# Moving the loads of batches 2 to 7 of a linear-attention + SiLU-MLP kernel from SyncE's queue to GpSimd's software queue

## The chip, the cores and the metric

One core of one Trainium2 chip. The metric is the device time of one launch in microseconds (us). Most executions of a kernel here agree within about 1%; every number compared below is from runs that were classed as fast, unless it says otherwise. A run of a version stands beside runs of the kernel before on the same chip.

A core has TensorE (PE in the profile; PEld is its weight load), VectorE (DVE), ScalarE (ACT), GpSimd (POOL) and SyncE (SP). A transfer is issued by one of these engines and is carried out by 16 DMA engines that all issuers share. Transfers issued by SyncE stand in one queue (q1 in the profile), those issued by GpSimd in another, the software queue (q0). A transfer lands when its completion is signalled; "issue to landing" runs from the start of its issue to that moment. A packet is one record of a DMA engine's work in the trace, with its queue, time and size.

## The reference

```
q, k, v: (8 batches, 8 heads, 576 rows, 64), float32
q_s = softmax of q over its last axis; k_s = softmax of k over the rows
kv  = einsum('bhsd,bhse->bhde', k_s, v)
x   = einsum('bhsd,bhde->bhse', q_s, kv)      # as 4608 rows of 512
h   = x @ w_in                                # 512 -> 2048
out = (h * sigmoid(h)) @ w_out                # 2048 -> 512, float32
```

## The kernel before

The tokens are worked in nine chunks of 512. `units` is a list of small pieces of matmul work (`mm1` for w_in, `mm2` for w_out); the attention work of batch `b` is placed into it at offsets from `begin[b]`. The order in which the code emits an engine's instructions is the order of that engine's program. The parts that matter:

```python
def load(b, name, src, ccs=None, eng=nc.sync):          # one of q, k, v: 1152 KB, rows of 2304 B
    if name not in st[b]:
        st[b][name] = ld.tile([128, NG, J * D], FP32, name=name)      # two buffers per name
    ...
    eng.dma_start(out=st[b][name][:, c, :], in_=x[:, c, :])

def tr_dma(b, eng):                                     # qT: the transposed exp(q), by DMA
    eng.dma_start_transpose(out=qt_tile(b)..., in_=st[b]["eq"]...)

# start: weights and batch 1 in GpSimd's queue (load_w1/load_w2: 1 MB float32 each, converted to bf16)
load_w1(0); load_w1(1); load_w2(0); load_w1(2)
load(1, "qt", q, eng=nc.gpsimd); load_w2(1); load_w1(3)
load(1, "kt", k, eng=nc.gpsimd); load_w2(2); load(1, "vt", v, eng=nc.gpsimd); load_w2(3)
...
def plan_attn(b, u, sm, vs, tp, ks, ox, eng=nc.gpsimd):
    # exp, sum and norm of q at u+sm[0:2] (norm on GpSimd), exp of k at u+sm[2:4], cast of v at u+vs
    ...
    plan(u + tp, lambda: tr_dma(b, nc.sync))
    if b == 1:
        plan(u + vs[0] + 1, lambda: load_behind(2))
    if b + 2 < B:
        at_ = u + max(tp, vs[1]) + 1
        plan(at_, lambda: [load(b + 2, *x) for x in (("qt", q), ("kt", k), ("vt", v))])
    # kv products at u+ks; xt(b, cc), the first users of qT(b), at u+ox
    ...
def load_behind(b):     # a one-element copy into the q tile: batch 2's loads must wait for the cast of v of batch 1
    st[b]["qt"] = ld.tile([128, NG, J * D], FP32, name="qt")
    nc.vector.tensor_copy(st[b]["qt"][0:1, 0, 0:1], vaug[(b - 1) % 2][0:1, J - 1, D:E1])
    for x in (("qt", q), ("kt", k), ("vt", v)):
        load(b, *x)
```

So SyncE's queue carries, in this order: batch 0's loads, the transpose of batch 1, the loads of batches 2 and 3, eight stores of chunk 0, the transpose of batch 2, the loads of batch 4, eight stores, and so on.

The softmax here doesn't subtract the row's maximum and nothing guards it: scores larger than these inputs give would overflow.

Of the kernel before, what the change touches and what calls it, by code (L numbers as in the profile page):

```python
# [8 lines left out]
FP32 = mybir.dt.float32  # L9
# [7 lines left out]
def kernel(  # L17
# [13 lines left out]
    nc = tc.nc  # L31
    B, H, S, D = q.shape
# [3 lines left out]
    J = S // P  # L36
    NG = H // 2
# [7 lines left out]
    E1 = D + 1  # L45
# [6 lines left out]
    vaug = [glob.tile([128, J, NG * E1], BF16, name=f"vaug{i}") for i in range(2)]  # L52
# [7 lines left out]
    ld = ctx.enter_context(tc.tile_pool(name="ld", bufs=2))  # L60
# [5 lines left out]

    st = [dict() for _ in range(B)]

    def load(b, name, src, ccs=None, eng=nc.sync):
        if name not in st[b]:  # L70
            st[b][name] = ld.tile([128, NG, J * D], FP32, name=name)
        x = src[b].rearrange("(g r) (p j) d -> g (r p) (j d)", r=2, j=J).rearrange("g x y -> x g y")
        c = slice(0, NG) if ccs is None else slice(2 * ccs, 2 * ccs + 2)
        eng.dma_start(out=st[b][name][:, c, :], in_=x[:, c, :])  # L74

    def jgd(t, cc):
        return t[:, 2 * cc:2 * cc + 2, :].rearrange("p g (j d) -> p j g d", d=D)
# [1 line left out]
    def exp(b, src, dst, cc):  # L79
        if dst not in st[b]:  # L80
            st[b][dst] = ap.tile([128, J, NG * D], BF16, name=dst)
        o = st[b][dst][:, :, cc * 128:(cc + 1) * 128].rearrange("p j (g d) -> p j g d", d=D)
        nc.scalar.activation(out=o, in_=jgd(st[b][src], cc), func=ACT.Exp)  # L83

    def vcast(b, cc, eng):
        o = vaug[b % 2].rearrange("p j (g e) -> p j g e", e=E1)[:, :, 2 * cc:2 * cc + 2, 0:D]
        if eng is nc.scalar:
            eng.copy(out=o, in_=jgd(st[b]["vt"], cc))  # L88
        else:
            eng.tensor_copy(o, jgd(st[b]["vt"], cc))  # L90

    def qsum(b, cc):
        if "zq" not in st[b]:
            st[b]["zq"] = ap.tile([128, 2, J, 2], FP32, name="zq")
            st[b]["rzq"] = ap.tile([128, 2, J, 2], FP32, name="rzq")
        e = st[b]["eq"][:, :, cc * 128:(cc + 1) * 128].rearrange("p j (g d) -> p j g d", d=D)
        nc.vector.reduce_sum(out=st[b]["zq"][:, cc], in_=e, axis=AX.X)  # L97
        nc.vector.reciprocal(out=st[b]["rzq"][:, cc], in_=st[b]["zq"][:, cc])

    def qnorm(b, cc, eng):  # L100
        e = st[b]["eq"][:, :, cc * 128:(cc + 1) * 128].rearrange("p j (g d) -> p j g d", d=D)
        r = st[b]["rzq"][:, cc]
        eng.tensor_tensor(  # L103
            out=e, in0=e, in1=r[:, :, :, None].to_broadcast([128, J, 2, D]), op=ALU.mult
        )
# [7 lines left out]
    def tr_dma(b, eng):  # L113
        eng.dma_start_transpose(
            out=qt_tile(b).rearrange("x j c y -> x (j c) y"),
            in_=st[b]["eq"].rearrange("x j y -> x (j y)"),
        )
# [20 lines left out]
    def kv(b, cc):  # L138
        t = [ps.tile([128, 512], FP32, name="kvps", tag="ring", bufs=PSB["ring"]) for _ in range(2)]
        st[b]["kvps", cc] = t  # L140
        for j in range(J):
            for r in range(2):
                nc.tensor.matmul(  # L143
                    out=t[r][:, 0:2 * E1],
                    lhsT=st[b]["ek"][r * P:(r + 1) * P, j, cc * 128:(cc + 1) * 128],
                    rhs=vaug[b % 2][r * P:(r + 1) * P, j, cc * 2 * E1:(cc + 1) * 2 * E1],
                    start=(j == 0),
                    stop=(j == J - 1),
                )

    def kvcopy(b, cc):
        for r in range(2):
            kp = st[b]["kvps", cc][r]
            rz = ap.tile([128, 2], FP32, name="rz", bufs=4)
            nc.vector.reciprocal(out=rz, in_=kp[:, D:2 * E1:E1])  # L155
            for g in range(2):
                h = slice(g * 64, (g + 1) * 64)
                nc.vector.tensor_scalar_mul(  # L158
                    out=kvn[b % 3][h, cc, r, :],
                    in0=kp[h, g * E1:g * E1 + D],  # L160
                    scalar1=rz[h, g:g + 1],
                )
# [3 lines left out]
    def xt(t, cc, tags=("ring", "ring"), dve=0):  # L166
        if t not in XT:
            XT[t] = mp.tile([128, NC, S], BF16, name="XT")
        for i, (off, size) in enumerate(part[t]):
            o1 = [  # L170
                ps.tile([128, TCH], FP32, name="o1", tag=tags[i], bufs=PSB[tags[i]])
                for _ in range(2)
            ]
            a = first = cut[t] + off
            while a < first + size:
                b, col = divmod(a, S)
                n = min(S - col, first + size - a)
                for g in range(2):
                    for r in range(2):
                        h = slice(g * 64, (g + 1) * 64)  # L180
                        nc.tensor.matmul(
                            out=o1[g][r * 64:(r + 1) * 64, a - first:a - first + n],
                            lhsT=kvn[b % 3][h, cc, r, :],
                            rhs=st[b]["qT"][h, col // P:(col + n) // P, cc, r * P:(r + 1) * P],
                        )
                a += n
            for g in range(2):
                x = XT[t][:, 2 * cc + g, off:off + size]
                if g < dve:
                    nc.vector.tensor_copy(x, o1[g][:, 0:size])  # L190
                else:
                    nc.scalar.copy(out=x, in_=o1[g][:, 0:size])  # L192
# [70 lines left out]
    for cc in range(2):  # L263
        load(0, "qt", q, cc)
    for cc in range(2):
        load(0, "kt", k, cc)
        load(0, "vt", v, cc)
# [7 lines left out]
    def load_w1(i):  # L275
        nc.gpsimd.dma_start(  # L276
            out=W1[:, :, i * FQ:(i + 1) * FQ],
            in_=w_in[:, i * FQ:(i + 1) * FQ].rearrange("(c p) f -> p c f", p=128),
        )

    def load_w2(i):
        nc.gpsimd.dma_start(  # L282
            out=W2[:, i * 4:(i + 1) * 4, :],
            in_=w_out[i * FQ:(i + 1) * FQ, :].rearrange("(fc p) o -> p fc o", p=128),
        )
# [3 lines left out]
    load_w1(1)  # L289
    load_w2(0)  # L290
    load_w1(2)
    load(1, "qt", q, eng=nc.gpsimd)
    load_w2(1)
    load_w1(3)
    load(1, "kt", k, eng=nc.gpsimd)
    load_w2(2)
    load(1, "vt", v, eng=nc.gpsimd)
    load_w2(3)

    wps = ps.tile([128, 512], FP32, name="wps", tag="ops", bufs=PSB["ops"])  # L300

# [43 lines left out]
    begin = {t: next(u for u, f in enumerate(units) if f[0] == ("mm1", t)) for t in range(NCH)}  # L345
    at = [[] for _ in units]

    def plan(u, f):
        at[u].append(f)

    def plan_attn(b, u, sm, vs, tp, ks, ox, eng=nc.gpsimd):



        for cc in range(2):
            plan(u + sm[cc], lambda cc=cc: exp(b, "qt", "eq", cc))
            plan(u + sm[cc] + 1, lambda cc=cc: (qsum(b, cc), qnorm(b, cc, nc.gpsimd)))
        for cc in range(2):
            plan(u + sm[2 + cc], lambda cc=cc: exp(b, "kt", "ek", cc))
            plan(u + vs[cc], lambda cc=cc: vcast(b, cc, eng))  # L360
        plan(u + tp, lambda: tr_dma(b, nc.sync))
        if b == 1:
            plan(u + vs[0] + 1, lambda: load_behind(2))
        if b + 2 < B:
            at_ = u + max(tp, vs[1]) + 1
            plan(at_, lambda: [load(b + 2, *x) for x in (("qt", q), ("kt", k), ("vt", v))])
        for cc in range(2):
            plan(u + ks[cc], lambda cc=cc: kv(b, cc))
            plan(u + ks[cc] + 1, lambda cc=cc: kvcopy(b, cc))
        for cc in range(2):  # L370
            plan(u + ox[cc], lambda cc=cc: xt(b, cc))

    def load_behind(b):

        st[b]["qt"] = ld.tile([128, NG, J * D], FP32, name="qt")
        nc.vector.tensor_copy(st[b]["qt"][0:1, 0, 0:1], vaug[(b - 1) % 2][0:1, J - 1, D:E1])
        for x in (("qt", q), ("kt", k), ("vt", v)):
            load(b, *x)

    V = nc.vector  # L380
    plan_attn(1, begin[1], (-20, -19, -11, -10), (-6, -5), -12, (-4, -3), (-2, 0), V)
    plan_attn(2, begin[2], (-23, -21, -18, -15), (-13, -12), -15, (-10, -7), (-5, -3))
    for b in range(3, B):
        plan_attn(b, begin[b], (-40, -36, -32, -28), (-34, -30), -20, (-15, -11), (-7, -4))
    for cc in range(2):
# [36 lines left out]
```

## Time and profile before

| | before |
|---|---|
| median of three runs | 296.51 us (296.35 to 297.26) |
| span of the profiled run | 294.7 us |
| TensorE busy | 281.8 us, 96% |
| GpSimd busy | 52.0 us, 18% |
| transpose of batch 1, issue to landing | 9.3 us |
| transposes of later batches | 4.7 to 4.9 us, that of batch 6 6.2 us |

The page of the kernel before. The strips cut the span into 40 slices of 7.4 us; a digit is the busy share in tenths, PEclk is the granted TensorE clock in tenths.

```profile
span 294.7 us, 4438 instructions
PE 281.8 (96%) x1682; PEld 132.6 (45%) x1682; DVE 164.1 (56%) x340; ACT 152.6 (52%) x250; POOL 52.0 (18%) x44
PE   8689999997999999999999999999999999999992
PEclk9999999998899999999999999999999999999999
DMA  7999999999949903892299218001800140023006
```

TensorE is the limit: apart from fill and tail its strip dips only in slice 10, about 66 to 74 us, and there the clock dips too. The DMA engines are full for the first 80 us and have room afterwards. The timeline of TensorE at the dip (start, duration, operation; in brackets the idle time ahead of it and what ended it):

```profile
69.82 0.24 PE L181 MATMUL o_980<-qT,kvn_63 64*64 64x128 bf16 x2
71.22 0.24 PE L181 MATMUL o_981<-qT,kvn_63 64*64 64x128 bf16 x2 [1.16 <-DVE kvn_64 L158]
72.01 0.44 PE L181 MATMUL o_980<-qT,kvn_64 64*64 64x384 bf16 x2 [0.54 <-DMA qT<-eq]
```

TensorE stood 1.16 us for a VectorE copy (kvn, the scaled kv product that `xt` multiplies with) and 0.54 us for the transpose of batch 2. The transpose was late because of what stands ahead of it in SyncE's order. SyncE's timeline (SPq is its issuing):

```profile
44.95 0.37 SPq L74 DMA_DIRECT2D qt<-in_q_dram  x1
...
50.45 2.75 SPq L74 DMA_DIRECT2D vt<-in_v_dram  x1
53.25 13.71 SPq L254 DMA_DIRECT2D out_dram<-ost  x8
67.07 3.13 SPq L114 DMA_TRANSPOSE qT<-eq  x1
```

Six loads, then eight stores whose issue took 13.71 us, then the transpose, whose input had been ready since 62.2 us. Of the 13.71 us, 6.0 us are waits of the last three stores for the landings of q, k and v of batch 3 (1.1, 2.5 and 2.4 us). They read nothing that these loads write: in the trace each of the three stores signals on the same semaphore as the load that it waits for, and waits for it first. This order in SyncE's queue is what the change sets out to remove.

The transpose of batch 1 is in time here. SyncE's issue, the landing line of the tile qT in this stretch, and TensorE's first `xt` of batch 1, with no idle time ahead of it:

```profile
36.87 6.33 SPq L114 DMA_TRANSPOSE qT<-eq  x1
...
DMA to landing us min/median/max: 9.3/9.3/9.3
...
47.34 0.38 PE L181 MATMUL o_712<-qT,kvn_63 64*64 64x448 bf16 x2
```

### The profile page before, as it was taken

To read this page: it belongs to the slowest core of one execution; us is meant where nothing else is said; L and a number is where in the kernel's file an instruction comes from. 1 tells how busy PE (TensorE), PEld (TensorE's weight loads), DVE (VectorE), ACT (ScalarE), POOL (GpSimd) and SP (SyncE) were. 2 spreads that over 40 slices of the span, in tenths; PEclk is the share of its full clock that TensorE was granted. 3 is DMA by queue.
4 is the path that set the end of the run, shared out by engine and by line. 5 is a ranking of instruction groups with operands and counts; after the bars stand their busy time and mean duration, and the time that the engine had idled before them with its cause. 6 is when DMAs were issued, how large, how long until landed. Compare 5 with 4: busy or idle time off the path is not lost.

```text
span 294.7 us, 4438 instructions
## 1 busy us (share of the span) xinstructions
PE 281.8 (96%) x1682; PEld 132.6 (45%) x1682; DVE 164.1 (56%) x340; ACT 152.6 (52%) x250; POOL 52.0 (18%) x44
## 2 busy tenths in 40 slices
PE   8689999997999999999999999999999999999992
PEld 3356654443444444444444444444444444444440
DVE  3985856758455665566556654756473543344421
ACT  5665664944662576358634863386325433553330
POOL 0641500172320035002500250025000000000000
PEclk9999999998899999999999999999999999999999
DMA  7999999999949903892299218001800140023006
GB/s 262 275 201 281 297 254 297 393 393 215 395 104 205 397 20 71 162 374 103 56 183 389 78 41 183 0 1 39 187 1 2 36 107 2 0 59 83 2 0 142
DMA packets 38309, 46.36 MB, mean 157 GB/s; under 512 B 18064, under 2 KB 22160, under 8 KB 38288
## 3 DMA queue, kind: packets, MB, share of 16 engines
q1 hardware_dynamic: 33248, 38.35, 44.7%
q0 software_dynamic: 5040, 7.73, 11.8%
q8 instruction: 13, 0.21, 0.3%
q14 instruction: 8, 0.07, 0.1%
HBM read 36.70 MB, written 9.44 MB: 157 GB/s over the span
## 4 chain that ended last, share of the span: by engine, by line
PE 76%; DMA 17%; POOL 2%; SPq 1%; DVE 1%; ACT 1%; issue 0%; ACTq 0%
PE ops L235 37%; PE hps L200 34%; DMA vt<-in_v_dram 8%; DMA W_59<-in_moe_w_out_dram 8%; PE kvps L143 3%; DMA qT<-eq 2%; POOL W_58 L276 1%; SPq L74 1%; POOL W_59 L282 1%; ACT XT L192 0%; DVE GT L216 0%; POOL qt L74 0%; DVE vaug_61 L90 0%; DVE ost L248 0%; POOL kt L74 0%
## 5 line engine op out<-in xcount | busy, mean ns | idle before, releaser
L216 DVE SCALAR_TENSOR_TENSOR GT<-sg,hps 128x512 bf16<-128x512 f32 (+2 forms) x176 | 99.5, 584 | 112.7 <-ACT sg L208 111.8
L200 PE MATMUL hps<-XT,W_58 128*128 128x512 bf16 (+3 forms) x640 | 147.6, 359 | 0.5 <-DVE XT L190 0.3
L235 PE MATMUL ops<-W_59,GT 128*128 128x512 bf16 x576 | 147.7, 381 | 0.2 <-DMA W_59<-in_moe_w_out_dram 0.2
L208 ACT ACTIVATE sg<-hps 128x512 f32<-128x512 f32 (+3 forms) x160 | 87.8, 554 | 111.0 <-PE hps L200 106.3
L200 PEld LDWEIGHTS <-W_58 128*128 128x128 bf16 x640 | 62.2, 98 | 65.8 <-issue 3.6
L235 PEld LDWEIGHTS <-GT 128*128 128x128 bf16 x576 | 54.7, 98 | 63.9 <-issue 2.8
L103 POOL TENSOR_TENSOR eq<-eq,rzq 128x1152 bf16<-128x1152 bf16 x14 | 29.6, 2117 | 138.7 <-ACT sg L208 102.0
L97 DVE TENSOR_REDUCE zq<-eq 128x18 f32<-128x1152 bf16 x16 | 21.5, 1345 | 4.3 <-ACT eq L83 4.3
L83 ACT ACTIVATE eq<-qt 128x1152 bf16<-128x1152 f32 x16 | 18.5, 1164 | 2.6 <-DMA qt<-in_q_dram 2.6
L83 ACT ACTIVATE ek<-kt 128x1152 bf16<-128x1152 f32 x16 | 18.5, 1158 | 1.7 <-DMA kt<-in_k_dram 1.7
L250 ACT ACTIVATE ost<-ops 128x512 f32<-128x512 f32 x18 | 10.7, 597 | 9.9 <-PE ops L235 8.8
L248 DVE TENSOR_SCALAR ost<-ops 128x512 f32<-128x512 f32 x18 | 12.3, 685 | 4.1 <-PE ops L235 4.1
L143 PEld LDWEIGHTS <-ek 64*128 64x128 bf16 x288 | 8.5, 93 | 8.8 <-issue 5.0
L304 PE MATMUL wps<-warm 128*128 128x512 bf16 x32 | 8.9, 428 | 1.2 <-DVE warm L260 1.2
L143 PE MATMUL kvps<-vaug_60,ek 64*128 64x130 bf16 x144 | 5.7, 217 | 1.9 <-ACT vaug_60 L88 1.7
L158 DVE TENSOR_SCALAR kvn_63<-kvps,rz 64x64 bf16<-64x64 f32 x24 | 6.8, 283 | 0.7
L158 DVE TENSOR_SCALAR kvn_62<-kvps,rz 64x64 bf16<-64x64 f32 x24 | 6.8, 283 | 0.6
L90 POOL CAST vaug_61<-vt 128x1152 bf16<-128x1152 f32 x6 | 6.8, 1159 | 0.0
L90 POOL CAST vaug_60<-vt 128x1152 bf16<-128x1152 f32 x6 | 6.8, 1156 | 0.0
L304 PEld LDWEIGHTS <-warm 128*128 128x128 bf16 x32 | 3.3, 109 | 5.2 <-issue 1.7
L155 DVE RECIPROCAL rz<-kvps 128x2 f32<-128x2 f32 x32 | 5.3, 165 | 0.6
L143 PE MATMUL kvps<-vaug_61,ek 64*128 64x130 bf16 x144 | 5.5, 217 | 0.1
(135 smaller groups left out, 78.0 us busy)
## 6 DMA issues: line engine op xcount, KB each, us to landing
out_dram<-ost SPq DMA_DIRECT2D x72, 128.0 KB, 2.3
qt<-in_q_dram SPq DMA_DIRECT2D x6, 1152.0 KB, 6.1
kt<-in_k_dram SPq DMA_DIRECT2D x6, 1152.0 KB, 8.9
vt<-in_v_dram SPq DMA_DIRECT2D x6, 1152.0 KB, 11.6
W_58<-in_moe_w_in_dram POOLq DMA_DIRECT2D x4, 512.0 KB, 10.3
W_59<-in_moe_w_out_dram POOLq DMA_DIRECT2D x4, 512.0 KB, 18.9
qt<-in_q_dram SPq DMA_DIRECT2D x2, 576.0 KB, 4.2
kt<-in_k_dram SPq DMA_DIRECT2D x2, 576.0 KB, 7.8
```

The source lines that it names most:

```text
L83: nc.scalar.activation(out=o, in_=jgd(st[b][src], cc), func=ACT.Exp)
L90: eng.tensor_copy(o, jgd(st[b]["vt"], cc))
L97: nc.vector.reduce_sum(out=st[b]["zq"][:, cc], in_=e, axis=AX.X)
L103: eng.tensor_tensor(out=e, in0=e, in1=r[:, :, :, None].to_broadcast([128, J, 2, D]), op=ALU.mult)
L143: nc.tensor.matmul(out=t[r][:, 0:2 * E1], lhsT=st[b]["ek"][r * P:(r + 1) * P, j, cc * 128:(cc + 1) * 128], rhs=vaug[b % 2][r * P:(r + 1) * ...
L158: nc.vector.tensor_scalar_mul(out=kvn[b % 3][h, cc, r, :], in0=kp[h, g * E1:g * E1 + D], scalar1=rz[h, g:g + 1],)
L200: nc.tensor.matmul(out=hps[:, 0:size], lhsT=W1[:, c, fb * 128:(fb + 1) * 128], rhs=XT[t][:, c, off:off + size], start=(c == 0), stop=(c == ...
L208: nc.scalar.activation(out=sg[:, 0:size], in_=hps[:, 0:size], func=ACT.Tanh, scale=0.5)
L216: nc.vector.scalar_tensor_tensor(out=GT[g][:, fb, col:col + n], in0=sg[:, h], scalar=1.0, in1=hps[:, h], op0=ALU.add, op1=ALU.mult,)
L235: nc.tensor.matmul(out=OP[t, tb], lhsT=GT[t][:, fc, tb * 128:(tb + 1) * 128], rhs=W2[:, fc, :], start=(fc == 0), stop=(fc == NFB - 1),)
L248: nc.vector.tensor_scalar_mul(out=ost, in0=OP[t, tb], scalar1=0.5)
L304: nc.tensor.matmul(out=wps, lhsT=warm[:, 0:128], rhs=warm, start=True, stop=True)
```

## The change

The loads of batches 2 to 7 join those of batch 1 in GpSimd's queue, so that SyncE keeps only batch 0's loads, the stores and the transposes. The hold on batch 2's loads (`load_behind`) goes, since in one queue they stand behind batch 1 and the weights anyway. Batch 2's plan offsets shift slightly, and the loads of batches 5 to 7 are emitted ten units earlier, ahead of the transpose instead of behind it (offset -29 instead of -19).

```diff
-    def load(b, name, src, ccs=None, eng=nc.sync):
+    def load(b, name, src, ccs=None):
...
-        eng.dma_start(out=st[b][name][:, c, :], in_=x[:, c, :])
+        (nc.gpsimd if b else nc.sync).dma_start(out=st[b][name][:, c, :], in_=x[:, c, :])
...
     load_w2(3)
+    load(2, "qt", q)
+    load(2, "kt", k)
...
-        if b == 1:
-            plan(u + vs[0] + 1, lambda: load_behind(2))
         if b + 2 < B:
-            at_ = u + max(tp, vs[1]) + 1
-            plan(at_, lambda: [load(b + 2, *x) for x in (("qt", q), ("kt", k), ("vt", v))])
+            plan(u + vs[1] + 1, lambda: [load(b + 2, *x) for x in (("qt", q), ("kt", k), ("vt", v))])
...
-    def load_behind(b): ...
...
     plan_attn(1, begin[1], (-20, -19, -11, -10), (-6, -5), -12, (-4, -3), (-2, 0), V)
-    plan_attn(2, begin[2], (-23, -21, -18, -15), (-13, -12), -15, (-10, -7), (-5, -3))
+    plan(begin[1] - 17, lambda: load(2, "vt", v))
+    plan_attn(2, begin[2], (-24, -21, -17, -14), (-15, -14), -14, (-10, -7), (-5, -3))
```

More of the change, by code (lines that the diff above doesn't have):

```diff
@@ L291 @@
     load_w1(2)
-    load(1, "qt", q, eng=nc.gpsimd)
+    load(1, "qt", q)
     load_w2(1)
     load_w1(3)
-    load(1, "kt", k, eng=nc.gpsimd)
+    load(1, "kt", k)
     load_w2(2)
-    load(1, "vt", v, eng=nc.gpsimd)
+    load(1, "vt", v)
     load_w2(3)
+    load(2, "qt", q)
+    load(2, "kt", k)
     wps = ps.tile([128, 512], FP32, name="wps", tag="ops", bufs=PSB["ops"])
@@ L371, in plan_attn @@
             plan(u + ox[cc], lambda cc=cc: xt(b, cc))
-    def load_behind(b):
-        st[b]["qt"] = ld.tile([128, NG, J * D], FP32, name="qt")
-        nc.vector.tensor_copy(st[b]["qt"][0:1, 0, 0:1], vaug[(b - 1) % 2][0:1, J - 1, D:E1])
-        for x in (("qt", q), ("kt", k), ("vt", v)):
-            load(b, *x)
     V = nc.vector
     plan_attn(1, begin[1], (-20, -19, -11, -10), (-6, -5), -12, (-4, -3), (-2, 0), V)
-    plan_attn(2, begin[2], (-23, -21, -18, -15), (-13, -12), -15, (-10, -7), (-5, -3))
+    plan(begin[1] - 17, lambda: load(2, "vt", v))
+    plan_attn(2, begin[2], (-24, -21, -17, -14), (-15, -14), -14, (-10, -7), (-5, -3))
     for b in range(3, B):
```

## The prediction

> **What bounds the kernel now.** TensorE. The page shows PE busy 281.8 of 294.7 us; the table of stretches shows 10.0 of every 10 us busy from 80 us to the tail. Besides fill and tail the only loss is at 70 to 76 us. The timeline shows TensorE idle 1.16 us (for kvn) and 0.54 us (for qT of batch 2), then eight matmuls at half clock (3.27 us instead of 1.7): about 3.5 us in all. The chain of waits leads there through six SyncE loads issued at 45 to 53 us, eight stores that wait for their landings, and SyncE's transpose at 67.07 us, whose input was ready at 62.2 us.
>
> **What the change does.** It moves 18 loads of 1152 KB from SyncE to GpSimd: 18 x 0.78 us of issue = 14 us more on an engine 18% busy, in its gaps. It removes one tiny copy. Batch 2's transpose no longer sits behind those loads, so the 3.5 us should go. Matmul work is unchanged.
>
> **What it costs.** The batch 1 transpose (issued 36.9 us) must land by 47.3 us, where TensorE multiplies with it; it lands at 46.2 us, 9.3 us after issue, against 4.7 to 4.9 us elsewhere. Packet records say why: while the software queue was full (40.5 to 42 us) it moved 33, 68 and 96 packets of 256 B per half microsecond beside 89, 80 and 74 of that queue; once that had drained, over 500. So the queues take turns packet by packet, as the Trainium skill states ("DMA: Bandwidth & Descriptors", section "Queues, rings and completion order"); this trace agrees. A transpose has 2304 such packets; a packet of a q, k or v load has 4608 B and takes 178 ns.
>
> Now the software queue ends at about 44 us. After the change q and k of batch 2 stand in it by 28 us, v and q of batches 2 and 3 from 37 us, k at 40, v of batch 3 at 45: six loads, 7.08 MB, behind the weights. At about 360 GB/s they last to about 63 us. One transpose packet per load packet is about 80 per us (estimate: 16 engines / (178 + 31 ns)), so the transpose ends with the backlog, at 55 to 65 us. TensorE is in order and stands from 47.3 us for 8 to 17 us, then restarts at half clock (3.4 us windows, as the clock record shows at 72 us): about 2 us more.
>
> Later batches: loads for b+2 follow the casts directly, about 9 us earlier (83 instead of 92.5 us), and overlap the transposes (89.6, 120.8, 149.6 us). Slack is 6 to 7 us beyond the usual 4.8 us landing; I estimate 3 to 6 us of delay: 0 to 2 us lost in all.
>
> **Sum.** 296.5 - 3.5 + about 14 + 2 + 2 = 311 us; range 300 to 319. Faster by over 2%: 0.02; within 2%: 0.10; slower: 0.88.
>
> **Right or wrong shows as.** The batch 1 transpose over 15 us to landing; one TensorE wait for "DMA qT" of 8 us or more near 47 us in the list of waits; half clock after it; no wait at batch 2; GpSimd busy near 66 us; the software queue with about 29 MB.
>
> **What would make it wrong.** If the engines share by time or bytes, the transpose lands by 50 us: a small stall, and the saving decides (294 to 297 us). If loads reach the queue later, or GpSimd blocks on semaphores, the stall is shorter. If batches 4 and 5 stall too, it is slower than 319.

## The result

The changed kernel takes 315.04 us (median of six runs, 313.56 to 315.47) against 296.4 us (294.98 to 297.26). The ratio is 1.0625, with a 95% interval of 1.0593 to 1.0657: 6% slower. Here and below a ratio is the mean time of one kernel's fast runs over that of the other's of the same rounds, so it is not quite the ratio of the medians.

The page of the changed kernel (slices of 7.8 us):

```profile
span 312.8 us, 4431 instructions
PE 284.8 (91%) x1682; PEld 133.5 (43%) x1682; DVE 164.3 (53%) x339; ACT 152.7 (49%) x250; POOL 65.4 (21%) x62
PE   8799991069989999999999999999999999999992
PEclk9979997559999999999999999999999999999998
DMA  7999999951492990199029702700450050014005
```

TensorE has a hole in slices 7 and 8 (PE 1 and 0), and its clock is halved in slices 8 and 9. The list of TensorE's waits in the changed kernel (total us, times, longest us) names it:

```profile
PE o_711 L181 <- DMA qT<-eq: 17.0, 1, 17.0
PE kvps L143 <- ACT vaug_60 L88: 1.6, 2, 0.8
```

One wait of 17.0 us, for the transpose of batch 1. The timeline around it, first TensorE, then SyncE's issue of that transpose and the landing line of the tile qT in this stretch:

```profile
47.00 1.04 PE L235 MATMUL ops<-W_59,GT 128*128 128x512 bf16 x4
65.05 0.58 PE L181 MATMUL o_711<-qT,kvn_63 64*64 64x448 bf16 x2 [17.01 <-DMA qT<-eq]
```

```profile
37.80 15.79 SPq L114 DMA_TRANSPOSE qT<-eq  x1
...
DMA to landing us min/median/max: 27.1/27.1/27.1
```

Issued at 37.8 us, landed at 64.9 us: 27.1 us instead of 9.3. Its issue alone held SyncE for 15.79 us. Meanwhile the software queue was being filled by GpSimd:

```profile
24.75 0.75 POOL L74 DMA_DIRECT2D qt<-in_q_dram  x1 [2.09 <-ACT sg L208]
27.74 0.75 POOL L74 DMA_DIRECT2D kt<-in_k_dram  x1 [2.24 <-DMA qt<-in_q_dram]
...
37.72 0.79 POOL L74 DMA_DIRECT2D vt<-in_v_dram  x1
38.50 0.75 POOL L74 DMA_DIRECT2D qt<-in_q_dram  x1
41.04 0.75 POOL L74 DMA_DIRECT2D kt<-in_k_dram  x1 [1.79 <-ACT ek L83]
45.72 0.75 POOL L74 DMA_DIRECT2D vt<-in_v_dram  x1 [3.93 <-DVE rz L155]
```

These are q, k, v of batch 2 and q, k, v of batch 3. The trace also records every packet of every queue. Counted per 2 us (stretch, packets of the software queue with their main size, packets of 256 B of the transpose):

```
stretch us   before: q0, transpose          changed: q0, transpose
40 to 42     337 (1024 B), 173              385 (1024 B),   2
42 to 44      81 (1024 B), 764              170 (4608 B), 148
44 to 46       0,         1367              161 (4608 B), 176
46 to 58     (transpose has landed)         160 to 162 (4608 B), 163 to 176 in each
58 to 60                                    161 (4608 B), 166
60 to 62                                     87 (4608 B), 562
```

From 46 to 58 us the two queues moved 80 and 85 packets per us: turn and turn about, though one packet has 4608 B and the other 256 B. The table leaves out packets of 4 B, of which the software queue had 61 in this stretch; with them the two queues moved 1025 and 1024 packets, so the turns are even. The transpose has 2304 packets, and it moved fast only once the software queue had run dry, or nearly so.

The half clock that follows is in the table of stretches (us busy in each 10 us, number of instructions, then PEclk, DMA share, GB/s). Three rows of the changed kernel:

```profile
50.00:60.00 10.00, 0.00 (x0) 0.00 (x0) 0.29 (x1) 0.00 (x0) 0.00 (x0) 0.53 1.05 391
60.00:70.00 10.00, 4.95 (x18) 1.51 (x19) 0.69 (x1) 1.85 (x4) 0.00 (x0) 0.50 0.70 135
70.00:80.00 10.00, 10.00 (x50) 4.73 (x49) 6.93 (x11) 7.86 (x14) 2.35 (x2) 0.95 0.17 38
```

The clock record of the trace has half clock from 50.5 to 71.0 us. Of that, TensorE worked from 65.05 us, about 6 us. What it cost can be read off the same matmuls in both kernels: from the first `xt` of batch 1 to the start of the next chunk's `xt` they took 22.48 us before (47.34 to 69.82) and 24.79 us now (65.05 to 89.84), 2.3 us more.

Where the 18.1 us between the two profiled spans lie can be read off the moments at which TensorE reaches the same matmuls (all from the two timelines):

| stage | before | changed | difference |
|---|---|---|---|
| ready for the first `xt` of batch 1 | 47.34 | 48.04 | +0.7 |
| wait for qT of batch 1 | 0 | 17.01 | +17.0 |
| from there to `xt` of batch 2 | 24.67 long | 26.21 long | +1.5 (half clock +2.3; then 0.8 less, of which the wait for qT of batch 2, now gone, is 0.54) |
| from there to `xt` of batch 3 | 29.61 long | 28.02 long | -1.6 (the half clock of the kernel before is gone) |
| from there to the end | 193.1 long | 193.5 long | +0.4 |

### The profile page after: what moved, and what is told of

Its sections match the earlier page's. It is cut to its first block, busy times and chain, and to the rows that moved or that the text cites. A ratio compares the mean times of both kernels' runs of the same rounds, so it can differ in the third digit from the quotient of the medians.

```text
span 312.8 us, 4431 instructions
## 1 busy us (share of the span) xinstructions
PE 284.8 (91%) x1682; PEld 133.5 (43%) x1682; DVE 164.3 (53%) x339; ACT 152.7 (49%) x250; POOL 65.4 (21%) x62
## 3 DMA queue, kind: packets, MB, share of 16 engines
q0 software_dynamic: 9936, 28.97, 29.4%
## 4 chain that ended last, share of the span: by engine, by line
PE 81%; DMA 12%; DVE 3%; SPq 1%; POOL 1%; ACT 1%; issue 0%; POOLq 0%; ACTq 0%; DVEq 0%
PE hps L200 38%; PE ops L235 38%; DMA qT<-eq 9%; DMA vt<-in_v_dram 3%; PE kvps L143 2%; DVE zq L97 1%; SPq L74 1%; POOL eq L103 1%; DVE GT L216 1%; DVE kvn_64 L158 1%; ACT vaug_60 L88 0%; DVE kvn_62 L158 0%; DVE rzq L98 0%; DVE ost L248 0%; DVE rz L155 0%
## 5 line engine op out<-in xcount | busy, mean ns | idle before, releaser
L248 DVE TENSOR_SCALAR ost<-ops 128x512 f32<-128x512 f32 x18 | 12.3, 686 | 23.0 <-PE ops L235 23.0
L306 PE MATMUL wps<-warm 128*128 128x512 bf16 x32 | 10.0, 470 | 1.2 <-DVE warm L260 1.2
L181 PEld LDWEIGHTS <-kvn_63 64*64 64x64 bf16 x48 | 1.5, 107 | 22.1 <-issue 20.3
L143 PE MATMUL kvps<-vaug_60,ek 64*128 64x130 bf16 x144 | 5.7, 217 | 1.8 <-ACT vaug_60 L88 1.6
```

The lines of the kernel that those rows point to most:

```text
L143: nc.tensor.matmul(out=t[r][:, 0:2 * E1], lhsT=st[b]["ek"][r * P:(r + 1) * P, j, cc * 128:(cc + 1) * 128], rhs=vaug[b % 2][r * P:(r + 1) * ...
L248: nc.vector.tensor_scalar_mul(out=ost, in0=OP[t, tb], scalar1=0.5)
```

## The experiments

**Theory A**: the DMA engines take turns between queues packet by packet. A backlog of large packets in another queue stretches the transpose, TensorE needs it and stands. **Rivals**: the software queue or GpSimd's issuing is slow in itself (B); only the loads of batch 3 matter (C); late loads or memory traffic in general hold TensorE (D); the transpose gets a fixed share of time or bytes (E); any traffic, whatever queue, slows it (F); only the software queue competes (G).

### hold_b3: half of the backlog

```diff
+    def hold(b, c):          # one element of qT(b), read by GpSimd: what follows waits for the transpose
+        nc.gpsimd.tensor_copy(gate[:, c:c + 1], st[b]["qT"][0:1, 0, 0, 0:1])
...
-            plan(u + vs[1] + 1, lambda: [load(b + 2, *x) ...])
+            plan(u + vs[1] + 1, lambda: (hold(1, 1) if b == 1 else None, [load(b + 2, *x) ...]))
```

> The changed kernel, with the three loads of batch 3 (not those of batch 2) held back on GpSimd until the transpose of batch 1 has landed. Theory A (the transpose gets one 256 B packet per software-queue packet for as long as that queue has a backlog, so it lands when the backlog ends): backlog behind the weights is halved (q, k, v of batch 2, 3.54 MB), ends near 54 us, transpose lands near 56 us instead of 64.9, TensorE waits 7 to 9 us instead of 17.0, time 304 to 308 us. Rival B (the software queue, or GpSimd's issuing, slows the transpose whatever stands in it; or the moved late loads cost the time): wait stays near 17 us, time near 315. Rival C (early batch 2 loads are harmless, only batch 3's hurt): no wait, about 296.

Measured: 306.14 us, ratio 1.0335 (1.0301 to 1.0369). The transpose landed 19.9 us after its issue at 36.74 us, that is at 56.6 us. TensorE's wait:

```profile
PE o L181 <- DMA qT<-eq: 7.9, 1, 7.9
```

All as theory A has it: half of the backlog, less than half of the wait. B, as the cause of the 17 us, and C fall: with the same queue the wait halved, and batch 2's loads alone cost 7.9 us. From 44 to 50 us the queues moved 79 and 83 packets per us.

### hold_b23: no backlog at batch 1

```diff
-    load(2, "qt", q)
-    load(2, "kt", k)
...
-            plan(u + vs[1] + 1, lambda: [load(b + 2, *x) ...])
+            if b == 1:
+                plan(u + vs[1] + 1, lambda: hold(1, 1))
+            plan(u + vs[1] + 1, lambda: [load(i, *x) for i in ((2, 3) if b == 1 else (b + 2,)) ...])
...
-    plan(begin[1] - 17, lambda: load(2, "vt", v))
```

> The changed kernel, still with all 21 loads of batches 1 to 7 in GpSimd's queue, but all six loads of batches 2 and 3 held back until the transpose of batch 1 has landed. Theory A: transpose of batch 1 lands 9 to 10 us after issue as in the kernel before (46 to 47 us), no wait of 17 us, no half-clock stretch after it; the backlog then lasts to about 67 us and overlaps the transpose of batch 2, which may lose 0 to 3 us; time 294 to 299 us. Rival B (GpSimd's queue or its 14 us of extra issue time is itself the cost): time stays above 305 us.

Measured: 307.83 us (median of the three fast runs), ratio 1.0399 (1.0344 to 1.0455); one of the four runs was slow, 313.32 us, and is left out. The expectation missed by 9 us. Theory A was right about batch 1 (landed 8.3 us after issue, no wait) and I was wrong about batch 2: the stall had moved there. TensorE's wait, then SyncE's and GpSimd's issues in order:

```profile
PE o L181 <- DMA qT<-eq: 9.9, 1, 9.9
```

```profile
62.58 7.54 SPq L114 DMA_TRANSPOSE qT<-eq  x1
```

```profile
50.52 0.76 POOL L74 DMA_DIRECT2D vt<-in_v_dram  x1
...
64.70 0.80 POOL L74 DMA_DIRECT2D qt<-in_q_dram  x1
65.50 0.75 POOL L74 DMA_DIRECT2D kt<-in_k_dram  x1
66.24 0.75 POOL L74 DMA_DIRECT2D vt<-in_v_dram  x1
```

The six held loads occupied the queue into the transpose's time (the last landed 21.1 us after its issue, at 71.6 us), and batch 4's three loads joined it at 64.7 us, two microseconds after the transpose of batch 2 had been issued. So that transpose met a backlog to about 79 us and landed 19.5 us after its issue. From 68 to 78 us the queues moved 80 and 85 packets per us, the same pair of numbers as at batch 1 of the changed kernel. I had counted only the backlog that was there when the transpose started, not what would be added.

### pe_transpose: the backlog stays, its victim goes

```diff
-        plan(u + tp, lambda: tr_dma(b, nc.sync))
+        if b == 1:       # 18 TensorE transposes, VectorE copies
+            for g, at_ in enumerate((tp + 2, tp + 4, tp + 6)):
+                plan(u + at_, lambda g=g: (tr(1, g), trcopy(1, g)))
+        else:
+            plan(u + tp, lambda: tr_dma(b, nc.sync))
```

> The changed kernel with all loads exactly where the change puts them, but qT of batch 1 made by TensorE (18 transposes of 128x128 and 4 VectorE copies, as for batch 0) instead of by the DMA transpose. The victim is removed, the backlog stays. Theory A: software queue still drains near 63 us, but no wait of 17 us and no half-clock stretch: 294 to 299 us (about 2 us of extra TensorE work included). Rival D (late landing of the loads themselves, or memory traffic in general, is what holds TensorE): a wait of several us stays and the time is above 303.

Measured: 296.36 us, ratio 1.0007 (0.9979 to 1.0034). The software queue still held loads until about 63 us and the loads stand where the change puts them; no wait for qT is left in TensorE's list, and no half clock after it. The list begins with 1.2 us:

```profile
PE wps L306 <- DVE warm L260: 1.2, 1, 1.2
```

So the loads' own landing and the traffic in general (D) do not hold TensorE. The 17 us went through the transpose of batch 1 and nothing else. The rest of the change, batch 2's offsets, the earlier late loads and GpSimd's extra issues, is all in this version too, so it cost nothing that these runs show.

### bf16_b17: the same bytes in smaller packets

```diff
-            st[b][name] = ld.tile([128, NG, J * D], FP32, name=name)
+            if b:
+                st[b][name] = ld.tile([128, NG, J * D], BF16, name=name + "h")
+            else:
+                st[b][name] = ld.tile([128, NG, J * D], FP32, name=name, bufs=1)
```

> The changed kernel, with the loads of batches 1 to 7 converted to bf16 on the way into SBUF. The same bytes are read, but a software-queue packet should have 1152 B instead of 4608 B, so the same backlog should have about twice to four times as many packets. Rounds inputs to bf16, so errors are larger. Theory A (turns are taken by packet): while both queues are full the transpose moves 140 to 170 packets per us instead of about 84, lands at 54 to 58 us instead of 64.9, TensorE waits 6 to 10 us instead of 17.0, time 303 to 308. Rival E (a fixed share of time or bytes for the transpose): rate stays near 84 per us, wait near 17 us, time near 315.

Measured: 309.97 us, ratio 1.0462 (1.0414 to 1.0511), correct against the reference. TensorE's waits for qT, of which 11.3 us is the one at batch 1 (0.5 and 0.8 us are at batches 4 and 5):

```profile
PE o L184 <- DMA qT<-eq: 12.6, 3, 11.3
```

The packets had 1152 B, and from 44 to 58 us the queues moved 139 and 144 packets per us (80 and 85 with packets of 4608 B); with those of 4 B counted it was 2016 and 2015 packets in all. That rejects a fixed share (E): the rate of the transpose follows the packet rate of the queue beside it, one for one. The landing, 59.3 us, was 1.3 us later than my range and the wait of 11.3 us longer than the 10 I allowed, because I had credited the transpose with too many packets before 44 us. It also corrects my picture: here the transpose ended before the backlog did (that lasted to about 64 us). It lands when its 2304 packets have had their turns, or soon after the other queue is empty, whichever is first.

### hold_split: no backlog at batches 1 and 2

Loads in three groups: q, k, v of batch 2 and q of batch 3 behind the transpose of batch 1; k, v of batch 3 and batch 4 behind that of batch 2; the rest as in the changed kernel.

```diff
-    load(2, "qt", q)
-    load(2, "kt", k)
...
+            if b <= 2:
+                plan(u + vs[1] + 1, lambda: hold(b, b))
+            if b == 1:   todo = [(2, q_), (2, k_), (2, v_), (3, q_)]
+            elif b == 2: todo = [(3, k_), (3, v_), (4, q_), (4, k_), (4, v_)]
+            else:        todo = [(b + 2, q_), (b + 2, k_), (b + 2, v_)]
+            plan(u + vs[1] + 1, lambda: [load(i, *x) for i, x in todo])
...
-    plan(begin[1] - 17, lambda: load(2, "vt", v))
```

> The changed kernel, all loads of batches 1 to 7 still in GpSimd's queue, but arranged so that no load stands in that queue while the transposes of batches 1 and 2 are in flight: q, k, v of batch 2 and q of batch 3 are held until the transpose of batch 1 has landed; k, v of batch 3 and all of batch 4 until that of batch 2 has. Theory A (the stall follows the backlog: at batch 1 in the changed kernel, at batch 2 when only batch 1 was protected): both transposes land in 5 to 10 us, no TensorE wait for qT above 1 us, time 293.5 to 296.5, that is 0 to 1% faster than before. Rival B (GpSimd's queue cannot feed this kernel): above 300.

Measured: 297.09 us, ratio 1.0041 (1.0004 to 1.0078), just above my range. The transposes of batches 1 and 2 landed in 7.8 and 5.4 us, as expected; the remaining wait, 1.9 us, was at batch 3 (landed after 14.1 us), again the first transpose that was not protected. (The profiled run, 299.59 us, is the slowest of the six, so its wait may be longer than the usual one.) **hold_split_kv** also moved the kv products of batch 2 earlier:

```diff
-    ... (-15, -14), -14, (-10, -7), (-5, -3))
+    ... (-15, -14), -14, (-11, -9), (-5, -3))
```

> As hold_split, and the kv products of batch 2 one and two units earlier, so that the copies that free their PSUM tiles come before TensorE needs those tiles. Expected: the 1.2 us wait of TensorE for kvn at batch 2, which the kernel before and all versions so far show, is gone; about 1 us below hold_split, 292.5 to 295.5.

Measured: 298.3 us, ratio 1.0069 (1.0037 to 1.0101), where I expected 1 us less than hold_split; that it is slower is not clear of the noise, as the intervals overlap. The wait for kvn did go, but TensorE then came to the transpose of batch 3 earlier (98.5 instead of 100.8 us in the profiles), and its wait for it was 3.3 us instead of 1.9. Time saved ahead of a transfer that lands late was not saved here.

### hold_all: each load behind a transpose

As hold_split, with the hold for every batch that has loads to issue, and hold and loads emitted behind the transpose:

```diff
-            if b <= 2:
-                plan(u + vs[1] + 1, lambda: hold(b, b))
+            plan(u + max(tp, vs[1]) + 1, lambda: hold(b, b) ...)
...
-            plan(u + vs[1] + 1, lambda: [load(i, *x) for i, x in todo])
+            plan(u + max(tp, vs[1]) + 1, lambda: [load(i, *x) for i, x in todo])
```

> All 21 loads of batches 1 to 7 in GpSimd's queue, each group held until the transpose that precedes it has landed, for every batch (hold_split did so for batches 1 and 2 only and lost 1.9 us at batch 3). Theory A: every transpose from batch 3 on lands in 4.6 to 6 us, no TensorE wait for qT over 0.5 us, time 294 to 296, as fast as the SyncE version without hold within 0.4%: the software queue itself costs nothing. Rival B (the software queue costs by itself): stays at 297 or above.

Measured: 295.02 us, ratio 0.9955 (0.9923 to 0.9987). All 21 loads are in the software queue, which moved the same 28.97 MB as in the changed kernel; the transposes from batch 2 on landed in 4.7 to 5.5 us (that of batch 6 in 6.3, against 6.2 in the kernel before), and no wait for qT is in TensorE's list:

```profile
PE o L181 <- DVE kvn L158: 1.9, 3, 1.2
PE kvps L143 <- ACT vaug L88: 1.3, 2, 0.8
PE wps L304 <- DVE warm L260: 1.2, 1, 1.2
PE kvps L143 <- DVE kvn L158: 0.2, 1, 0.2
```

So the software queue and GpSimd's issuing (B) cost nothing by themselves that this run shows. It differs from the changed kernel, by 20 us, only in where the loads stand beside the transposes, and in the one-element holds that keep them there.

### sync_no_hold: the kernel before without its hold

```diff
-            plan(u + vs[0] + 1, lambda: load_behind(2))
+            plan(u + tp, lambda: [load(2, *x) for x in (("qt", q), ("kt", k), ("vt", v))])
```

> The kernel before, loads still on SyncE, but the one-element copy that holds batch 2's loads is gone: they are issued directly behind the transpose of batch 1, in the same queue. Theory A with one ring served in order: loads that stand behind the transpose in its own queue do not slow it (lands 46 to 47 us), loads start about 2 us earlier, the stores and the transpose of batch 2 too, and most of the 3.5 us lost at 70 to 76 us goes: 293 to 296. Rival F (any load traffic in flight slows a transpose, whatever the queue): TensorE waits several us for qT of batch 1, time above 299.

Measured: 294.47 us, ratio 0.9942 (0.9911 to 0.9973): 0.6% faster than before, the fastest median of all versions. Loads that stand behind the transpose in its own queue did not slow it (7.5 us to landing, F falls), although they were issued at once after it. The wait for qT of batch 2 and the half clock after it are gone. Why is only in part shown: the loads began 1.1 us earlier, not 2, and the transpose of batch 2 was issued only 0.3 us earlier (66.78 us), while in this profile TensorE came to the place 1.1 us later (70.91 instead of 69.82 us). What is left there is the 1.2 us for kvn:

```profile
PE o L181 <- DVE kvn L158: 1.4, 2, 1.2
```

**sync_no_hold_kv** then moved the second kv product of batch 2 one unit earlier (offsets -10, -7 to -10, -8).

> The best version so far (loads on SyncE, no hold) with the second kv product of batch 2 one unit earlier, so that the copies that free its PSUM tiles come before TensorE needs them. Expected: the 1.2 us wait for kvn at batch 2 gone, 0.5 to 1.5 us below sync_no_hold, about 293.3 (ratio to before 0.988 to 0.993). If something else ends last there, no change (294.5).

Measured: 294.71 us, ratio 0.9947 (0.9916 to 0.9977). In its profile that wait of 1.2 us is gone, but the time is the same within the noise. Its profiled run had other small waits (1.4 us in three pieces for w_out, 0.7 us for qT) that the other had not; whether they belong to the version or to the run stays open.

### late567 and late567_act: the late loads alone

In the kernel before, only the loads of batches 5, 6, 7 are moved, to GpSimd's queue or to ScalarE's:

```diff
-            at_ = u + max(tp, vs[1]) + 1
-            plan(at_, lambda: [load(b + 2, *x) ...])
+            at_ = u + (max(tp, vs[1]) if b < 3 else vs[1]) + 1       # late567_act: sm[3] in place of vs[1]
+            e = nc.sync if b < 3 else nc.gpsimd                      # late567_act: nc.scalar
+            plan(at_, lambda: [load(b + 2, *x, eng=e) ...])
```

> The kernel before, with only the loads of batches 5, 6 and 7 (9 of the 18 moved ones) in GpSimd's queue, at the changed kernel's place directly after the casts. Theory A: their transposes land in 11 to 13 us instead of 4.8, which the slack of 11 to 12 us just covers: no TensorE wait over 1 us, the time equal to before within 0.5%. Rival B (GpSimd's issue time or queue costs by itself): 1% or more slower.

Measured: 296.81 us, ratio 1.0029 (0.9992 to 1.0066): no difference that the interval shows. The transposes of batches 3 to 5 landed in 10.3 to 12.1 us instead of 4.8, and the slack took it: of the wait for qT in TensorE's list, 0.86 us is the one at batch 2 that the kernel before has as well, and 0.27 us is new. The packet counts correct the reason that I had given for the delay. At batch 4, from 120 to 126 us, SyncE's queue and the software queue moved about 26 and 32 packets per half microsecond (395 and 397 in all, with those of 4 B), but those of SyncE were 2048 B packets of the eight stores that stand ahead of the transpose in SyncE's queue; the transpose itself started only at about 126.5 us, when the loads were nearly done. So it was late mostly because the stores ahead of it were.

> As late567, but the loads of batches 5, 6 and 7 are issued by ScalarE, so in a second hardware queue instead of the software queue. Theory A (any other ring takes turns packet by packet): while loads and SyncE's stores and transpose are both queued, the two rings move equal numbers of packets; load packets are 2304 B here, half of the software queue's, so a transpose beside them gets 130 to 160 packets per us instead of 80 to 88. Rival G (only the software queue competes): transposes land in 4.8 us as before. Time equal to before within 0.5%.

Measured: 295.92 us, ratio 1.0 (0.9953 to 1.0048). The transposes of batches 3 to 5 landed in 10.3, 7.7 and 8.0 us, so a second hardware queue competes too, and G falls. Beside stores the counts were about 39 to 50 per half microsecond, not equal as I had expected; but with the packets of 4 B counted, SyncE's and ScalarE's queues moved 195 and 194 packets from 120 to 122 us and 206 and 210 from 150 to 152 us. The transpose itself met the load queue in full for one half microsecond only (73 and 77 packets at batch 5). So two hardware queues look to take turns too; that the turns are strict is not shown by stretches as short as these.

## Why the prediction was right

The measured 315.04 us lies inside the range of 300 to 319 and 4 us above the point. Point by point:

- *Turns packet by packet.* Right, and the core of it. The Trainium skill says in "DMA: Bandwidth & Descriptors", section "Queues, rings and completion order", that each DMA engine goes round its queues at packet granularity. The trace agrees: 80 packets per us against 85 with 4608 B packets, and 139 against 144 with 1152 B packets; with packets of 4 B counted, 1025 against 1024 and 2016 against 2015. My estimate of 80 per us for the transpose was 5 too low.
- *The transpose lands at 55 to 65 us, TensorE stands from 47.3 us for 8 to 17 us.* It landed at 64.9 us; TensorE stood 17.0 us from 48.04 us. That is the edge of both ranges: the sum used 14 us and was 3 us short in this term, though the prediction's own end of the backlog, 63 us, would have given about 16.
- *Half clock after it, about 2 us.* Right: it cost 2.3 us.
- *The 3.5 us at batch 2 go.* Only in part. The place itself became 0.8 us shorter, 0.54 of it the wait for qT, and the half clock went (1.6 us between batches 2 and 3), 2.4 us in all; but the 1.17 us for kvn stayed, and stayed in most later versions. I had put it into the same episode although the timeline named another releaser for it. "No wait at batch 2" was therefore wrong for kvn.
- *Later batches lose 0 to 2 us.* 0.4 us. The transposes of batches 3 to 5 came 6 to 8 us later than before (11.2 to 12.3 us to landing), more than the 3 to 6 I gave, but the slack held. The mechanism was mis-told: the stores ahead of them in SyncE's queue were delayed.
- *GpSimd busy near 66 us, about 29 MB in the software queue.* 65.4 us and 28.97 MB.
- *Transposes elsewhere land in 4.7 to 4.9 us.* That of batch 6 took 6.2 us in the kernel before; nothing in the argument rests on it.

The terms of the sum that were mis-sized: the stall 3 us short, the half clock 0.3 us short, the saving at batch 2 1.1 us over (kvn), the late batches 1.6 us over, and 0.7 us before the stall not foreseen. Together they leave the point 3.5 us low; between the profiled spans it was 3.6 us, between the medians 4. That the late batches took back a part of the miss at the stall is luck; the mechanism is not.

What stays open: the changed kernel's profile has a half-clock stretch at 16 to 20 us which the profile of before has not. Other versions show it too, so I take it for a difference of runs, but did not test that. And between 62 and 64 us, with only 13 packets left in the software queue, the transpose moved just 202 packets; the same slow end is in the kernel before. In both, about one software-queue packet at a time was still under way then (1.0 on average from 62.25 to 64 us, 1.1 from 43 to 44.2 us in the kernel before), and once the last was gone the transpose ended, or, in the kernel before, went on at 567 packets per half microsecond. Why so small a rest holds it up is not shown.

## What to carry to other kernels

Moving a transfer to another queue takes away its wait for the transfers ahead of it, and with it the protection of those transfers: loads issued behind the transpose in its own queue did not delay it here (7.5 us to landing in sync_no_hold), loads in the other queue did, packet for packet (27.1 us). The transpose with its many small packets lost the more the larger the other packets were (85 per us beside 4608 B, 144 beside 1152 B). Before moving bulk loads, list each small-packet transfer with its deadline, and count the backlog that other queues will hold until then, including what will be added while it is in flight. If the loads must be elsewhere, hold each behind the landing of the transfer that it could delay, for every stage: protecting one stage moved the stall to the next one, twice.

## What the Trainium skill lacked or had wrong

- "DMA: Bandwidth & Descriptors", section "Queues, rings and completion order", has the turns at packet granularity, but not what follows for unequal packets. A packet takes one turn whatever its size, those of 4 B included (1025 against 1024 packets): a transpose of 256 B packets beside 4608 B packets took 27.1 us to landing, against 4.8 us with no other queue at work. The same page's "Rules for kernel authors" says that a transpose next to ordinary DMAs needs nothing; that may hold for correctness, but for time these runs differ by 20 us (315.04 against 295.02).
- The same page, section "Issuing engines are not separate DMA queues", says that issuing from several engines only saves the sequencer's issue time. Here it changed who waits for whom, by 6% of the kernel's time (ratio 1.0625).
- The same page, section "SWDGE vs HWDGE vs iDMA", gives a packet as 4096 B or less, preferably. The software queue's packet records here are larger than that, 4608 B, the size of two rows of 2304 B; SyncE's for the same loads have 2304 B.
- "TensorE: Matmul & The Clock Gate", section "Part 1: The HAM clock gate (the "warmup" mystery)", has the clock halve after at least one idle window of about 3.4 us. In the kernel before it halved for 3.4 us after waits of 1.16 and 0.54 us in close order, and in hold_split after one of 1.9 us; a wait of 1.2 us alone did not halve it (pe_transpose). For short waits the page has only a kernel that idles often between groups of matmuls. The length of the half-clock stretch, 3.4 us, agrees.
